# One PSUM pool of eight single banks, scores handled bank by bank, and an order planned from measured lengths, in a windowed-attention, gated-convolution and top-2 expert-attention kernel

## Chip, cores and metric

The kernel runs on one core of a Trainium2 chip. The metric is the device time of one execution in microseconds (us), as the median of several runs; lower is better. The engines of the core are called by the short names of the profile: PE (TensorE matmul), PEld (its weight loads), DVE (VectorE), ACT (ScalarE), POOL (GpSimd) and SP (SyncE, which here issues the DMAs). PSUM, into which PE writes, has eight banks of 128 partitions by 2 KB, that is 512 fp32 values per partition and bank.

## What is computed

Three steps on arrays of 8 batches, 8 heads, 576 positions and 64 values per head (512 values per position): attention in a window of 64 positions, a gated causal convolution, and four single-head causal attentions ("experts"), of which each position adds up the two with the highest logits.

```python
def _attn_ref(q, k, v):                 # 1: window attention, 8 x 8 x 576 x 64
    scores = np.matmul(q, k.transpose(0, 1, 3, 2)) / np.sqrt(D)
    scores = np.where((rel >= 0) & (rel < 64), scores, -1000000000.0)
    attn = np.exp(scores - np.max(scores, axis=-1, keepdims=True))
    attn = attn / (np.sum(attn, axis=-1, keepdims=True) + 1e-09)
    return np.matmul(attn, v)
def _moe_ref(x, w_val, conv_w, w_out):  # 2: x is 8 x 576 x 512
    for k in range(5):
        gate_pre += conv_w[k][None, None, :] * xp[:, k:k + S, :]
    gate = 1.0 / (1.0 + np.exp(-gate_pre))
    return gate * (x @ w_val) @ w_out
def _moe2_ref(x, w_gate, wq, wk, wv, wo):  # 3: E = 4 experts, 2 chosen
    topk = np.argpartition(-(x @ w_gate), 2, axis=-1)[..., :2]
    for e in range(E):
        scores = causal(scale * ((x @ wq[e]) @ (x @ wk[e]).transpose(0, 2, 1)))
        a = softmax(scores)             # with + 1e-9 in the denominator
        out += (weight of e, where chosen) * (a @ (x @ wv[e]) @ wo[e])
```

## The kernel before, in words

**Tiles and stages.** The positions of each batch are cut into five tiles (four of 128 rows and one of 64), so there are 40 tiles. Each tile goes through five functions, whose stages have short names that the text uses:

- front loads q, k and v (tiles raw and rv) and takes the largest magnitude of v (am, L593), from which a batch gets its scales.
- attn1 transposes q and k (qt, L669) and evicts them to qT and kT (qe); splits v into a high and a low fp16 half (vs, vh, vl) and copies the overlap of two tiles (vb); computes the banded scores (sp: the mask by L728, the fp32 products by L730); takes the maxima (mx, L737, negated); exponentiates head by head (ex, L744); splits the result into two fp16 halves in tile Phl (ph L275 or L279, pl L282); transposes it by DMA into PT; multiplies by v (pv, L795), normalises (xn), transposes (xt, L833) and evicts to xT (fp32) and xs (two fp16 halves, xh and xl).
- conv_gate makes the convolution on POOL (cv, L865 to L876: five products with the taps, four additions), tanh on ACT (th, L885), the product with w_val on PE (val, 48 matmuls at L894 to L896: high by high, low by high, high by low), the gate (gv, L902) and its two fp16 halves gs (gh, gl L911).
- proj multiplies by the prepared weights wproj (qk L927 to L929, 48 matmuls; v3 L945 to L947), evicts q3 and k3 (h3), V3 (v3h, v3l) and the logits (tile w4), and finds the two chosen experts and their weights by some ten small steps on DVE (rt, L997 to L1033).
- attn2 computes the causal scores of two or four experts at a time (s3, L1076), maxima (m3, L1085), exponentials with their sums (x3, L1090), the row factors (f3, L1099 and L1103), the two fp16 halves in tile P3hl (ph3 and pl3), the DMA transpose into P3T, the product with V3 (y, L1156), its two fp16 halves ys (yh on ACT L275, yl on DVE L282), the product with wo (o, L1181 to L1183 and L1177), the eviction to tile ot (ot, L275) and the store (st).

Ahead of and beside the first tiles, weights() turns the weights into scaled fp16 pairs. Since `gate * val @ w_out` goes linearly into the four experts, w_out is multiplied by wq, wk, wv and the gate weights once (L485 to L489) and only the product wproj is used. Each of the eight 128x512 pieces of w_val and w_out passes three steps on DVE (L372 to L374), one on ACT (L379) and two on POOL (L387, L388; called the guard here). 36 triples of idle matmuls (fill, L1204) stand at the lowest urgency wherever PE would wait, and 16 more follow the last scores.

**PSUM.** Eight banks are shared out to three kinds of tile: sc, two tiles of two banks each (scores of both attentions), tr, two single banks (transposes, and the outputs of pv and y), and pj, two single banks (the outputs of val, qk, v3, o, and fill).

**What sets the order.** Nothing is scheduled by the compiler: each engine works through its own list in order. The lists come from class Plan. Every stage of every tile is entered with its possible engines and lengths, what it reads and writes, and an urgency: `start[n] + OFF[stage] * STRETCH - BOOST`, with start from a period II = 14109.34 ns per tile. Plan.order then simulates a machine with these lengths and with as many buffers of each name as BUFS says, always takes the operation that can start first (and, among equals, the most urgent), and the operations are written out in the order of the simulated starts. The lengths come from formulas (dv, sa, pl, mm), with a charge of 1500 for choosing DVE and 500 for ACT where either can do it. A tile name in BUFS with the number 1 has one buffer, so that its next user waits for all readers of the last: before, Phl, PT and ot have one, P3hl, kT (a whole batch's keys) and ys two, q3, P3T and w4 three.

## Time and profile before

| | us |
|---|---|
| median of three runs (lowest to highest) | 673.25 (671.52 to 673.39) |
| span of the profiled execution | 668.4 |
| outside the span, against the median | 4.85 |
| PE busy in the span | 622.3 (93%) |
| DVE busy | 554.8 (83%) |
| ACT busy | 509.9 (76%) |
| POOL busy | 487.1 (73%) |

The span runs from the first to the last instruction of one profiled execution, which has no time of its own beside it on the page; so the 4.85 us are the median less the span. Busy time counts an instruction from its start to its end. On PE and DVE one instruction begins before the one ahead of it has ended, so the durations of neighbours overlap, and busy time is the time in which at least one is running. What an added or removed instruction is worth is therefore read from the distance between two starts, and a wait shorter than such an overlap isn't seen as idle time at all.

### The profile page before, as it was taken

What the parts mean: (1) busy time and instruction counts of PE and PEld (TensorE: products, weight loads), DVE (VectorE), ACT (ScalarE), POOL (GpSimd) and SP (SyncE); (2) the same over time, 40 slices, a digit from 0 to 9 for tenths busy, and PEclk for the clock granted to TensorE, in tenths of its full rate; (3) what the DMA queues carried; (4) which work ended last, traced back from release to release, by engine and by line L of the source; (5) the groups of instructions that cost most, each with busy time, mean ns of one, the idle gap of its engine ahead of it and who ended that gap; (6) DMA issues with size and microseconds to landing.
All of it is one profiled execution on the core that took longest, in us unless ns stands there. A gap on an engine that the chain in (4) does not pass through costs nothing. (4 is left out here: it accounts for less than half of the span.)

```text
span 668.4 us, 25309 instructions
## 1 busy us (share of the span) xinstructions
PE 622.3 (93%) x10241; PEld 486.1 (73%) x10253; DVE 554.8 (83%) x1663; ACT 509.9 (76%) x1320; POOL 487.1 (73%) x549
## 2 busy tenths in 40 slices
PE   8999979888989999999999999999999999998996
PEld 3556768777777777877887778877878788776753
DVE  9578788878879889888898989898888978986782
ACT  3568568977878868888788878888879788875662
POOL 6287798995977888669948895789768797867000
PEclk9999999989999999999999999999999999998999
DMA  9769645887796989598887789679647465644256
GB/s 256 197 180 233 153 92 113 205 153 121 134 223 115 170 138 216 124 170 141 169 185 159 126 181 190 142 145 172 151 110 154 97 128 103 110 104 97 50 118 128
DMA packets 306530, 99.44 MB, mean 149 GB/s; under 512 B 294362, under 2 KB 296942, under 8 KB 306414
## 3 DMA queue, kind: packets, MB, share of 16 engines
q1 hardware_dynamic: 306414, 97.84, 71.8%
q8 instruction: 80, 1.31, 0.8%
q14 instruction: 36, 0.29, 0.1%
HBM read 34.63 MB, written 9.44 MB: 66 GB/s over the span
## 5 line engine op out<-in xcount | busy, mean ns | idle before, releaser
L876 POOL TENSOR_TENSOR acc<-acc,ctmp 128x512 f32<-128x512 f32 (+1 forms) x160 | 186.6, 1166 | 6.3
L874 POOL TENSOR_TENSOR ctmp<-xT,cw 128x512 f32<-128x512 f32 (+1 forms) x160 | 152.4, 973 | 0.0
L744 ACT ACTIVATE sc<-sc,mx 128x128 f32<-128x128 f32 x288 | 98.7, 343 | 19.6 <-DVE mx L737 11.1
L894 PE MATMUL pj<-xs,wval 128*128 128x128 f16 (+1 forms) x640 | 101.9, 217 | 3.6 <-ACT k L275 1.4
L895 PE MATMUL pj<-xs,wval 128*128 128x128 f16 (+1 forms) x640 | 101.7, 217 | 0.0
L896 PE MATMUL pj<-xs,wval 128*128 128x128 f16 (+1 forms) x640 | 101.7, 216 | 0.0
L927 PE MATMUL pj<-gs,wproj 128*128 128x128 f16 (+1 forms) x640 | 99.6, 214 | 1.4 <-ACT ot L275 1.4
L928 PE MATMUL pj<-gs,wproj 128*128 128x128 f16 (+1 forms) x640 | 99.5, 214 | 0.0
L929 PE MATMUL pj<-gs,wproj 128*128 128x128 f16 (+1 forms) x640 | 99.5, 214 | 0.0
L1090 ACT ACTIVATE sc<-sc,mx 128x128 f32<-128x128 f32 (+3 forms) x144 | 76.0, 528 | 26.2 <-DVE mx L1085 23.4
L865 POOL TENSOR_TENSOR acc<-xT,cw 128x512 f32<-128x512 f32 (+1 forms) x34 | 34.3, 1010 | 73.7 <-issue 37.5
L282 DVE SCALAR_TENSOR_TENSOR P3hl<-sc,mx,P3hl 128x128 f16<-128x128 f32 (+3 forms) x144 | 75.3, 573 | 10.7 <-ACT P3hl L275 10.5
L275 ACT ACTIVATE P3hl<-sc,mx 128x256 f16<-128x256 f32 (+4 forms) x143 | 69.4, 558 | 9.9 <-DVE mx L1103 3.8
L1076 PE MATMUL sc<-k,q 64*128 64x128 f32 (+5 forms) x384 | 66.6, 450 | 5.5 <-DVE Phl L282 2.8
L691 POOL TENSOR_TENSOR VA<-rv,VA 128x512 f16<-128x512 f32 (+1 forms) x40 | 45.0, 1134 | 30.5 <-ACT VA L275 27.1
L895 PEld LDWEIGHTS <-wval 128*128 128x128 f16 x640 | 62.3, 99 | 3.2 <-issue 2.8
L894 PEld LDWEIGHTS <-wval 128*128 128x128 f16 x640 | 62.3, 99 | 2.9 <-DVE w L1033 1.2
L1085 DVE TENSOR_REDUCE mx<-sc 128x4 f32<-128x512 f32 (+3 forms) x64 | 61.7, 966 | 2.7 <-PE sc L1076 2.2
L927 PEld LDWEIGHTS <-wproj 128*128 128x128 f16 x640 | 61.4, 98 | 1.8 <-issue 0.7
L928 PEld LDWEIGHTS <-wproj 128*128 128x128 f16 x640 | 61.3, 98 | 1.7 <-issue 1.3
L896 PEld LDWEIGHTS <-wval 128*128 128x128 f16 x640 | 62.4, 99 | 0.0
L929 PEld LDWEIGHTS <-wproj 128*128 128x128 f16 x640 | 61.3, 98 | 0.0
(198 smaller groups left out, 1731.9 us busy)
## 6 DMA issues: line engine op xcount, KB each, us to landing
VB<-VA SPq DMA_DIRECT2D x64, 132.0 KB, 2.8
raw<-in_q SPq DMA_DIRECT2D x32, 256.0 KB, 3.5
rv<-in_v SPq DMA_DIRECT2D x32, 256.0 KB, 4.1
raw<-in_k SPq DMA_DIRECT2D x32, 256.0 KB, 3.8
out<-ot SPq DMA_DIRECT2D x32, 256.0 KB, 2.6
w<-in_moe_w_val SPq DMA_DIRECT2D x4, 512.0 KB, 4.0
w<-in_moe_w_out SPq DMA_DIRECT2D x4, 512.0 KB, 3.7
rv<-in_v SPq DMA_DIRECT2D x8, 128.0 KB, 3.7
```

The source lines that it names most:

```text
L275: ac.activation(o, i, AF.Copy, scale=scale)
L282: ve.scalar_tensor_tensor(o, i, scale, hi, op0=OP.mult, op1=OP.subtract)
L744: ac.activation(ps[:, i, :], ps[:, i, :], AF.Exp, bias=t[:, hh:hh + 1])
L874: po.tensor_mul(y, x[:, :, t + i:t + i + T], W["cw"][:, :, t + i:t + i + 1].to_broadcast([128, 4, T]))
L876: po.tensor_add(acc[:, :, :T], acc[:, :, :T], y)
L894: pe.matmul(p[:, m, :T], lhsT=w0, rhs=xs[:, 0, c, :T], start=c == 0, stop=False)
L895: pe.matmul(p[:, m, :T], lhsT=w0, rhs=xs[:, 1, c, :T], start=False, stop=False)
L896: pe.matmul(p[:, m, :T], lhsT=w1, rhs=xs[:, 0, c, :T], start=False, stop=c == 3)
L927: pe.matmul(p[:, m, :T], lhsT=w0, rhs=gs[:, 0, c, :T], start=c == 0, stop=False)
L928: pe.matmul(p[:, m, :T], lhsT=w0, rhs=gs[:, 1, c, :T], start=False, stop=False)
L929: pe.matmul(p[:, m, :T], lhsT=w1, rhs=gs[:, 0, c, :T], start=False, stop=c == 3)
L1090: ac.activation(ps[:, x], ps[:, x], AF.Exp, bias=mx[:, x:x + 1], accum_out=mx[:, 4 + x:5 + x])
```

## The change

**PSUM.** The three kinds become one pool, ps, of eight single banks. Only the planner knows of a limit per use: at most four banks for scores (qs), three for transposes, pv and y (qt), three for val, qk, v3, o and fill (qj).

**Scores bank by bank.** sp and s3 write two single banks where they wrote a tile of two. Maxima, fp16 halves and row factors are then made for each bank by itself, and the planner may put other work between the two; ex becomes one planner operation per head. The last tile of a batch, whose s3 scores are 576 wide, has 512 in one bank and 64 in the other, and two small steps that join the maxima (m3c) and the sums (f3s).

**Keys per tile.** kT holds the keys of one tile instead of a batch (three buffers). A product of sp that reaches over two tiles becomes two of 64 columns: 28 matmuls in place of 20 in the middle tiles of a batch, 20 in place of 12 in the last, 10 as before in the first.

**Buffers.** Phl, PT and ot go from one to two, P3hl, ys and kT to three, P3T to four, q3 to five, w4 to eight; ctmp goes from two tiles of 128x512 to one four times as large.

**Convolution, routing, guard.** Two taps become one POOL instruction of 1024 values, their sums another, and two additions join them to the first tap: six instructions per tile in place of nine, over as many values; the first tap is always on POOL (before, six of 40 tiles had it on ACT). The routing's addition of 1e-9 goes into its last step. vh is always on ACT. All guards are one step on DVE (L440 of the changed kernel), none is on POOL.

**Planner.** The lengths are constants per stage. Latencies (OV, WAIT), a window (NEAR) within which urgency decides among operations that could start, a table of some 900 corrections to the urgency (PRIO, by stage, by stage and tile in the batch, and by tile), a charge of 103.9 for DVE and of -147.2 for ACT, and II = 13700 replace the old numbers.

```diff
-BUFS = dict(raw=5, rv=9, qT=2, kT=2, VA=4, VB=2, Phl=1, PT=1, xn=2, xT=3, xs=2, acc=2, ctmp=2, gs=5,
-           P3hl=2, P3T=3, V3=7, q3=3, k3=2, ys=2, ot=1, am=2, scs=3, w4=3, sc=2, tr=2, pj=2,
-           w64=3, t1=3, wbig=1, ab=4, wp=1, wcat=1)
+BUFS = dict(raw=5, rv=9, qT=2, kT=3, VA=4, VB=2, Phl=2, PT=2, xn=2, xT=3, xs=2, acc=2, ctmp=1, gs=5,
+            P3hl=3, P3T=4, V3=7, q3=5, k3=2, ys=3, ot=2, am=2, scs=3, w4=8, ps=8,
+            w64=3, t1=3, wbig=1, wp=1, wcat=1)
...
+LIMIT = dict(qs=4, qt=3, qj=3)
-II = 14109.34
+II = 13700.0
...
+        's3': 101843.2, ('s3', 0): -2019.0, 'm3': 107663.2, ('m3', 0): 26351.9, 'x3': 144300.6, ('x3', 0): 507958.6, 'f3': -50072.1,
...
-BIAS = dict(DVE=1500.0, POOL=0.0, ACT=500.0)
+BIAS = dict(DVE=103.9, POOL=0.0, ACT=-147.2)
+OV = dict(PE=168.0, DVE=85.0, ACT=110.0, POOL=42.0)
+WAIT = dict(PE=146.0, DVE=34.0, ACT=34.0, POOL=100.0, SP=60.0)
...
+                    if j and (last or not x):
+                        w2 = ((o[:, 0:64], qq, T_["kT", n - 1][rs, m, 64:128]), (o[:, 64:128], qq, kT[rs, m, 0:64]))
+                    else:
+                        w2 = ((o, qq, kT[rs, m]),)
...
-        def mx():
-            T_["mx", n] = t = pool.tile([128, 8], F32, name="mx", bufs=5)
-            ve.tensor_reduce(t[:, :NH].rearrange("p (a b) -> p a b", a=2), s1v(), axis=AX.X, op=OP.max, negate=True)
+        def mx(r):
+            if ("mx", n) not in T_:
+                T_["mx", n] = pool.tile([128, 8], F32, name="mx", bufs=5)
+            ve.tensor_reduce(T_["mx", n][:, 4 * r:4 * r + NQ], T_["s1p", n, r][:, :NQ], axis=AX.X, op=OP.max, negate=True)
...
-        def pl_():
-            hl = T_["Phl", n]
-            residual(by_bank(hl[:, 1, :NH]), by_bank(s1v()), by_bank(hl[:, 0, :NH]), PS)
+        def pl_(r):
+            residual(part1(1, r), flat(T_["s1p", n, r][:, :NQ]), part1(0, r), PS)
...
+            xs = bass.AP(tensor=x.tensor, offset=x.offset + t, ap=[x.ap[0], [1, 2], x.ap[1], [1, T]])
+            ws = bass.AP(tensor=w.tensor, offset=w.offset + t, ap=[w.ap[0], [1, 2], w.ap[1], [0, T]])
+            po.tensor_mul(T_["ctmp", n][:, t - 1:t + 1, :, :T], xs, ws)
...
-            ps = bank(("s3p", n, g), [128, 1024])
+            ps = [bank(("s3p", n, g, u), [128, 512]) for u in (0, 1)]
```

**PE, the product o after its y.** These are the rows up to the first matmul of an o, in the middle of each list. Before, the rows in front of o belong to a val; the y that it needs lies hundreds of matmuls ahead.

```order
L895 LDWEIGHTS wval
L895 MATMUL pj<-xs,wval 128x128
L896 LDWEIGHTS wval
L896 MATMUL pj<-xs,wval 128x128
L1181 LDWEIGHTS ys
L1181 MATMUL pj<-wo_133,ys 128x512
```

After, at a place where y (L1240) of the same tile stands directly ahead: its last matmul, then the end of a small s3 (L1127), then o (L1265).

```order
L1240 LDWEIGHTS V_5_111
L1240 MATMUL ps<-P3T,V_5_111 64x128
L1127 MATMUL ps<-k_4830,q_5945 64x512 x2
L1127 MATMUL ps<-k_4830,q_5945 64x64 x2
L1127 LDWEIGHTS identb
L1127 MATMUL ps<-caus,identb 64x64
L1265 LDWEIGHTS ys
L1265 MATMUL ps<-wo_133,ys 128x512
```

Between the end of y and the first matmul of o, in which time ACT and DVE have to make ys, stood 287 to 448 matmuls in 30 of the 40 tiles; in the changed list there are 7 to 589, at most 30 in 11 tiles and at most 60 in 18.

**DVE, the scores of the window attention.** Before, the maxima of a tile's eight heads are one instruction over two banks (mx<-sc, L737), here next to the maxima of an s3 (L1085), a qT eviction and the routing of a tile (tile w).

```order
L1006 TENSOR_TENSOR pj<-pj,before 128x4x4
L1007 TENSOR_REDUCE pj<-pj 128x4
L737 TENSOR_REDUCE mx<-sc 128x8
L1085 TENSOR_REDUCE mx_6082<-sc 128x2
L279 TENSOR_SCALAR qT<-tr 128x512
L1015 SCALAR_TENSOR_TENSOR w_6004<-pj,w_6004 128x4
L846 TENSOR_TENSOR xs<-tr,xs 128x512
```

After, the maxima (L785) and the low halves (Phl, L332) come in two instructions of one bank each, with the gate (L955, L964), ys and xs between them.

```order
L785 TENSOR_REDUCE mx<-ps 128x4 x2
L332 SCALAR_TENSOR_TENSOR ys<-ps,ys 128x2x64
L329 TENSOR_SCALAR Phl<-ps 128x512
L332 SCALAR_TENSOR_TENSOR Phl<-ps,Phl 128x512
L955 SCALAR_TENSOR_TENSOR ps<-acc,ps 128x512
L332 SCALAR_TENSOR_TENSOR Phl<-ps,Phl 128x512
L785 TENSOR_REDUCE mx<-ps 128x4
L964 TENSOR_TENSOR gs<-ps,gs 128x512
L893 TENSOR_TENSOR xs<-ps,xs 128x4x64
```

The list of DVE grows from 1625 to 1855 rows, most of them such halves.

**The last piece of w_out, on POOL and on DVE.** Before, its guard is two instructions on POOL (L387, L388), between those of other pieces and the splitting of v.

```order
L387 TENSOR_SCALAR w_557<-w_557 128x512
L388 TENSOR_TENSOR t_613<-w_557,t_613 128x512
L589 MEMSET am 128x5
L387 TENSOR_SCALAR w_611<-w_611 128x512
L388 TENSOR_TENSOR t_656<-w_611,t_656 128x512
L691 TENSOR_TENSOR VA_102<-rv,VA_102 64x8x64
```

After, it is one instruction on DVE (L440), behind the three steps of the conversion (L422 to L424), with the scale of wo (so) between them.

```order
L422 TENSOR_SCALAR t_920<-w_780 128x512
L423 SCALAR_TENSOR_TENSOR t_920<-w_780,t_920 128x512
L424 SCALAR_TENSOR_TENSOR t_920<-w_780,t_920 128x512
L578 COPY cm<-ps 128x1
L382 TENSOR_SCALAR so<-cm 128x1
L383 TENSOR_SCALAR cscr<-so 128x1
L384 TENSOR_SCALAR so<-cscr 128x1
L387 TENSOR_SCALAR iso<-so 128x1
L785 TENSOR_REDUCE mx<-ps 128x4
L329 TENSOR_SCALAR wo_133<-w_592,so 128x512
L440 SCALAR_TENSOR_TENSOR t_920<-w_780,t_920 128x512
```

The POOL guards of all pieces leave POOL's list, and the load of that piece moves on SP's list from row 25 to row 43, behind 18 more issues.

## Rows read from the trace of the kernel before

**Rows 1.** The page: busy us, share of the span, instructions, per engine.

```profile
PE 622.3 (93%) x10241; PEld 486.1 (73%) x10253; DVE 554.8 (83%) x1663; ACT 509.9 (76%) x1320; POOL 487.1 (73%) x549
```

**Rows 2.** Windows: stretch, length, busy us (instructions) per engine, PE clock, DMA share, GB/s.

```profile
0.00:91.30 91.30, 81.20 (x686) 51.22 (x693) 69.42 (x141) 50.74 (x102) 61.65 (x68) 1.00 0.80 200
91.30:636.50 545.20, 517.24 (x9245) 422.55 (x9250) 469.22 (x1471) 444.36 (x1181) 424.96 (x478) 0.99 0.72 142
212.50:570.10 357.60, 346.44 (x6229) 280.51 (x6233) 314.29 (x976) 299.46 (x792) 285.64 (x320) 1.00 0.77 151
636.50:668.40 31.90, 23.83 (x314) 12.35 (x311) 16.18 (x53) 14.85 (x37) 0.47 (x4) 0.96 0.60 120
```

**Rows 3.** Timeline of PE, middle of val: start, duration (us), instruction.

```profile
339.15 0.23 PE L894 MATMUL pj<-xs,wval 128*128 128x128 f16 x1
339.21 0.22 PE L895 MATMUL pj<-xs,wval 128*128 128x128 f16 x1
```

**Rows 4.** Waits of PE, 91.3 to 636.5: waiting, awaited, total us, times, longest.

```profile
PE tr L795 <- DMA PT<-Phl: 2.9, 4, 1.2
PE sc L1076 <- DVE Phl L282: 2.8, 3, 1.3
PE tr L1156 <- DMA P3T<-P3hl: 2.8, 2, 2.4
...
PE sc L728 <- DVE P3hl L282: 1.4, 2, 1.2
PE pj L927 <- ACT ot L275: 1.4, 2, 1.1
PE pj L894 <- ACT k L275: 1.4, 3, 0.7
...
PE pj L894 <- ACT ot L275: 1.2, 1, 1.2
PE tr L1156 <- DVE xs L846: 1.0, 2, 0.5
```

**Rows 5.** Timeline of PE, an sp of a middle tile: mask, then products.

```profile
343.96 0.41 PE L728 MATMUL sc<-band_middle,twice 64*64 64x512 bf16 x4
344.20 1.04 PE L730 MATMUL sc<-kT,qT 64*64 64x128 f32 x32
```

**Rows 6.** Timeline of DVE: neighbours of 512 columns, and neighbours of 1024.

```profile
330.62 0.66 DVE L911 TENSOR_TENSOR gs<-pj,gs 128x512 f16<-128x512 f32 x1
331.20 0.41 DVE L846 TENSOR_TENSOR xs<-tr,xs 128x256 f16<-128x256 f32 x1
...
338.43 1.22 DVE L282 SCALAR_TENSOR_TENSOR Phl<-sc,Phl 128x1024 f16<-128x1024 f32 x1
339.57 1.22 DVE L1085 TENSOR_REDUCE mx<-sc 128x4 f32<-128x1024 f32 x1
```

**Rows 7.** Timeline, the last piece of w_out: load, guard, first qk.

```profile
45.62 0.35 SPq L364 DMA_DIRECT2D w<-in_moe_w_out  x1
...
55.89 1.97 POOL L387 TENSOR_SCALAR w<-w 128x512 f32<-128x512 f32 x1
57.94 1.30 POOL L388 TENSOR_TENSOR t<-w,t 128x512 f32<-128x512 f32 x1
...
91.31 0.22 PE L927 MATMUL pj<-gs,wproj 128*128 128x128 f16 x1
```

**Rows 8.** Waits of DVE, whole span.

```profile
DVE ys L282 <- ACT ys L275: 14.1, 13, 6.1
```

**Rows 9.** The chain that ended last, in order of time: start, us, what.

```profile
649.71 5.01 DMA P3T<-P3hl
...
656.17 3.58 DMA out<-ot
...
659.86 0.70 ACT ot L275
...
661.19 1.44 PE tr L1156 x60
```

More of the change, by code (lines that the diff above doesn't have):

```diff
@@ L110, in order @@
                 succ[d].append(i)
+        wait = [min(WAIT[x[0]] for x in o[1]) for o in self.ops]
         avail = [0.0] * n
[L112 removed]
         freed = {}
[L114 removed]
+        free = dict(PE=3300.0, DVE=5300.0, ACT=4300.0, POOL=1700.0, SP=700.0)
+        hw, cold, since, was = 0.0, COLD, set(), "f"
         ready = {i for i in range(n) if not missing[i]}
[L116 removed]
+        out = []
         while ready:
[L118 removed]
+            found = []
             for i in ready:
[L120 removed]
+                _, engs, fn, deps, use, svc = self.ops[i]
                 t, need = avail[i], {}
                 for key in use:
[L123 to L125 removed]
+                    if key not in since:
                         need[key[0]] = need.get(key[0], 0) + 1
@@ L1083, in m3 @@
-        def m3(g):
-            T_["mx3", n, g] = mx = late().tile([128, 12], F32, name="mx3", bufs=6)
-            ve.tensor_reduce(mx[:, :NX], view(g), axis=AX.X, op=OP.max, negate=True)
-        def x3(g):
-            mx, ps = T_["mx3", n, g], view(g)
-            for x in range(NX):
-                ac.activation(ps[:, x], ps[:, x], AF.Exp, bias=mx[:, x:x + 1], accum_out=mx[:, 4 + x:5 + x])
-        def part(g, i):
-            return T_["P3hl", n, g][:, i * wt:i * wt + w0].rearrange("p (x w) -> p x w", x=NX)
+        NU = 1 if last else NX // 2
@@ new lines, in parts3, with m3 @@
+        def parts3(g, u):
+            if last:
+                return ((u, 0, (0, 512)[u], (512, 64)[u]),)
+            return tuple((x, x % NU * pitch, x * wd, wd) for x in range(u * NU, u * NU + NU))
+        def m3(g, u):
+            if ("mx3", n, g) not in T_:
+                T_["mx3", n, g] = late().tile([128, 12], F32, name="mx3", bufs=6)
+            xs = parts3(g, u)
+            ps = T_["s3p", n, g, u]
+            v = ps[:, :xs[0][3]] if NU == 1 else ps.rearrange("p (x w) -> p x w", x=NU)[:, :, :wd]
+            ve.tensor_reduce(T_["mx3", n, g][:, u * NU:u * NU + NU], v, axis=AX.X, op=OP.max, negate=True)
@@ L1110, in pz3, with ph3 @@
+        def ph3(e, g, u):
+            if ("P3hl", n, g) not in T_:
+                new(("P3hl", n, g), [128, 2048], F16, late())
+            for h, l, p, f in split3(g, u):
+                copy(e, h, p, f)
         def pz3(g):
@@ L1113, in pz3, with pl3 @@
             po.memset(hl[:, 640 + 576:1280], 0.0)
[L1115 to L1117 removed]
+        def pl3(g, u):
+            for h, l, p, f in split3(g, u):
+                residual(l, p, h, f)
         def P3T(g):
@@ L1144, in y @@
+            if last:
+                op("pz", n, (("POOL", 170.0),), lambda g=g: pz3(g), r=[("P3hl", n, g, 0, 0)], w=[("P3hl", n, g, 2)])
+            op("P3T", n, (("SP", 900.0 + 50.0 * (2 * wt // 128)),), lambda g=g: P3T(g),
+               r=[("P3hl", n, g, i, u) for i in (0, 1) for u in (0, 1)] + ([("P3hl", n, g, 2)] if last else []),
+               w=[("P3T", n, g)], svc=160.0 * 2 * wt / 128)
         def y():
```

577 lines of the change are left out of this document (271 added, 306 removed), and 83 rows, old and new, of the table PRIO.

## The prediction

> **What bounds the kernel now.** I read the busy times first. PE is busy for 622.3 of 668.4 us, DVE for 554.8, and no other engine for more than 510 [rows 1]: PE is the bound as long as its work is at hand. Then the windows, cut where the program changes character [rows 2]. Until 91.3 us the weights are prepared and PE lacks 91.30 - 81.20 = 10.1 us (idle matmuls of fill count as busy there). From 91.3 to 636.5 it lacks 545.20 - 517.24 = 28.0 us, 11.2 of them in the five middle batches, each of which takes 357.60/5 = 71.5 us, with 346.44/5 = 69.3 us of busy PE. In the last 31.9 us it lacks 8.1. The granted clock is at its upper level, 2.4 GHz, in all of these (0.96 to 1.00), so no term for the clock stands below. The ceiling follows: if every visible gap vanished, 46 of 668.4 us would go, and no more than what is hidden besides.
>
> Something is hidden. A 128-column matmul lasts 0.22 us, but the next starts 0.06 us after it [rows 3], so a wait of up to 0.16 us between two of them shows as busy time. Each tile has some 13 places where PE starts another kind of work, 520 in all, and each may hide up to that much.
>
> Next, what the visible gaps wait for. In the list of PE's waits the eleven largest rows between 91.3 and 636.5, of which eight are shown, sum to 19.9 us. Six of them are waits for somebody to read a PSUM tile empty: scores behind Phl (2.8) and P3hl (1.4), qk and val behind ot or k in pj (1.4, 1.4, 1.2), y behind xs in tr (1.0), together 9.2 us [rows 4]. The largest others are waits for data, the transposing DMAs above all (2.9 and 2.8) [rows 4]. So about 9.2/19.9 = 46% of the sized waiting is for a bank, and the rest for a result.
>
> **The change, part by part.** *Banks.* Eight banks for anybody take away the waits in which the wrong kind of bank is free. I let the whole bank share go: 0.46 x 28.0 = 13 us. It cannot be under 0, if the waits for data take the places (each gap ends with the last of several things), and not over 28.0, if the new order and the doubled buffers meet the waits for data too. I take 13, since the two DMA rows have prices that more buffers alone don't change. *Hidden waits.* If half of the 520 places hide 0.08 us, that is 21 us; the bank share of it is 9.6. I take -4, between 0 and -15.
>
> *Products of sp.* In 32 tiles, eight products of 128 columns become sixteen of 64: eight matmuls more, of two records each. The 32 records of a middle sp take 1.04 us [rows 5], 0.033 each. Sixteen more at that price cost 0.52 us per tile, 17 us in all; if time goes with the columns, which stay the same, nothing. The nearest row, a 128-column fp16 matmul every 0.06 us [rows 3], speaks for time by columns, but not of pieces this short, so I take a third of the upper end, +6. All of this lies on PE, the bound, and no cover takes it.
>
> *Halves on DVE.* 230 more rows in its list, most of them half an instruction. Two neighbours of 512 columns start 0.58 us apart and two of 1024 start 1.14 us apart [rows 6]: a split costs 2 x 0.58 - 1.14 = 0.02 us by starts and 2 x 0.66 - 1.22 = 0.10 by durations. That makes 5 to 23 us on DVE, of which 357.6/668.4, or 3 to 12 us, fall in the five middle batches, where DVE is busy for 314.3 of 357.6 us [rows 2]: 88% become 89 to 91%. I cost it at nothing: the cover is the 43 us in which DVE idles there. If that cover is too thin, the price is rival two. In return the first half of a tile's scores can be exponentiated while the second is reduced, and each bank comes free by itself; that gain is inside the 13.
>
> Against this edit speaks the Trainium skill, page "Perfetto Trace Analysis", section "Optimizing Scalar/DVE Operations": larger instructions raise the throughput of an engine that is saturated, and a DVE instruction on PSUM carries about 125 ns of its own. By that figure the 230 halves would be an estimated 29 us on DVE instead of my 5 to 23; the starts in [rows 6] put the price near a sixth of the page's. The same section also allows the opposite, breaking instructions up where an engine that isn't saturated makes others wait; which of the two holds at 88% no row here shows.
>
> *Lead-in.* The first qk starts at 91.31, and behind it are the products of w_out. The guard of the last piece of w_out runs on POOL from 55.89 to 59.24, 3.3 us [rows 7]; one DVE instruction of 512 columns costs about 0.6 by [rows 6], so 2.7 us leave that path, if it is the one that sets 91.31. Against it stands the load: issued at 45.62 now, it moves behind 18 more issues of some 0.35 us [rows 7], 6.3 us later at worst. And 8 of the 10.1 idle us could go at best. I take -3, from +6 to -8.
>
> *Tail.* The chain that ended last has a transposing DMA of 5.01 us (P3T) and the store of an ot, 3.58 us, for which the only buffer of ot is awaited before the next ACT eviction, the last y behind it [rows 9]. A second ot lets that 3.58 go, a third P3hl part of the 5.01. What is late next is the arithmetic of the last tile, which is as long as before. I take -5, from 0 to -8.
>
> *At nothing.* POOL's taps: six instructions over the same values as nine, with six tiles' first tap added, on an engine that is busy for 425 of 545 us [rows 2]; the cover is the time of val on PE, since only the gate behind it needs tanh. Were it gone, the first tap would be late by one POOL instruction in each of six tiles. The routing without its addition, vh on ACT, and three-buffered kT have one answer each, nothing within what can be measured (a difference under about 0.3%, 2 us, can't be told from no change).
>
> *The sum.* -13 - 4 + 6 - 3 - 5 = -19. The span would be 668.4 - 19 = 649.4; the median is 4.85 above the span and I leave it so: 654 us. Its own range, 645 to 667, comes from moving the two largest unknowns, the bank share and sp, by some 10.
>
> **Rivals.** *One, deeper:* the new order also takes the waits for data, because it is planned with other lengths and there are second buffers for Phl and PT. Then all 28.0 us go, and 8 in the lead-in: 673.25 - 28 - 4 + 6 - 8 - 5 = 634. For it: half of the sized waits have buffers among their causes. Against it: no gap in a list of some 520 starts would be left.
>
> *Two, no change: DVE gives the gain back.* Should the halves cost 0.10 each, the middle batches hold 314.3 + 12 = 326 us of DVE; in five periods of 68.7 us, which the forecast has, that is 95%, and an in-order engine that full makes PE wait about as often as the banks did. The 17 us of the banks and hidden waits come back, and the result is 654 + 17 = 671, with a little more, 673. For it: 14.1 us in 13 waits of DVE for ys, the longest 6.1 [rows 8], show that its queue already stalls on ACT. Against it: the price by starts is 0.02. The rule of the Trainium skill on saturated engines ("Perfetto Trace Analysis", "Optimizing Scalar/DVE Operations") would give this outcome.
>
> *Three, slower: o meets ys late.* In the changed list 11 tiles have at most 30 matmuls between y and o, and 18 at most 60, where before nearly all had hundreds. PE works in order, so when o's ys isn't ready, everything behind it waits, however many banks are free. Behind y come an ACT eviction and then a DVE residual, and the wait of the latter for the former has a mean of 14.1/13 = 1.1 us and a longest of 6.1 [rows 8]. Thirty 128-column matmuls cover 30 x 0.06 = 1.8 us. With 1.8 us uncovered in the eleven tightest tiles and 1.1 in the other seven, 20 + 8 = 28 us are added: 654 + 28 = 682, own range 674 to 700. It decides as soon as the new waits exceed the 19 gained. For it: every other stage was moved by the same table, and any of them may be as tight. Against it: the rows between y and o in such places are often scores, whose 512-column fp32 products are longer than 0.06 apart, and ACT and DVE may have nothing ahead of ys at that moment.
>
> *Four, the change doesn't do what it says:* a limit known only to the planner might be outrun on the chip, so that bank waits stay. That gives 673 - 1 at best, and I count it with rival two.
>
> **How the numbers follow.** Chances: the forecast 0.50, deeper 0.15, no change 0.13, slower 0.22. The predicted time is the forecast's, 654. The range leaves out the lower half of rival one and the upper half of rival three: 637 to 684 holds 0.50 + 0.06 + 0.13 + 0.12, some 0.8. Faster by over 2 us means below 671.2: forecast and rival one with 0.65, and 0.05 of rival two, 0.70. Within 2 us: 0.05 of rival two and 0.02 of rival three, 0.07. Slower: the rest, 0.03 and 0.20, 0.23.
>
> **What would show it.** Banks: among PE's waits between the first qk and the last batch, rows released by Phl, P3hl, ot, k and xs shrink below 2 us together, and the middle period is 68 to 70 us. The products of sp: an sp of a middle tile takes 1.0 to 1.5 us. DVE: busy under 91% in the middle, and the maxima of 512 columns start 0.58 apart. Lead-in: the first qk before 90. Tail: no wait for ot in the last chain. The forecast is wrong if PE's waits for ys, Phl or xs as data are among its largest rows (rival three), if DVE is above 94% in the middle (rival two), or if PE idles under 8 us between the first qk and the last batch (rival one).

## Result and profile after

| | before | changed |
|---|---|---|
| median of five runs, us | 671.58 (669.55 to 673.39) | 664.17 (662.65 to 665.62) |
| ratio, 95% interval | | 0.990 (0.9867 to 0.9932) |
| span of the profiled execution | 668.4 | 660.9 |

The change makes the kernel faster by 1.0%, where 654 us, or 2.9%, had been forecast. The sign was right and 664 lies in the range; of the 19 us that were forecast, 7.4 came. The executions measured here take 1.7 to 2.2 us more than their own spans, most of them 1.8, so of the 4.85 us that the forecast put around the span some 3 were only this: the profiled execution of the kernel before was faster than its median.

The page of the changed kernel first, with the busy us, share and instructions per engine; it answers to [rows 1]:

```profile
PE 628.3 (95%) x10759; PEld 495.4 (75%) x10765; DVE 585.5 (89%) x1893; ACT 483.0 (73%) x1363; POOL 447.8 (68%) x417
```

Then its windows, with the columns of [rows 2], cut at the first and the last qk; the kernel before, cut at its own first and last qk, stands behind it.

```profile
0.00:102.60 102.60, 90.24 (x817) 58.28 (x823) 85.92 (x170) 52.41 (x115) 36.69 (x46) 0.95 0.79 183
102.60:635.30 532.70, 518.10 (x9662) 425.96 (x9661) 484.08 (x1672) 416.80 (x1213) 410.67 (x368) 1.00 0.78 144
635.30:660.90 25.60, 19.96 (x289) 11.13 (x284) 15.48 (x53) 13.74 (x37) 0.47 (x4) 0.94 0.73 150
```

```profile
91.30:637.90 546.60, 518.64 (x9293) 423.95 (x9297) 470.59 (x1474) 444.89 (x1183) 424.96 (x478) 0.99 0.72 142
637.90:668.40 30.50, 22.43 (x270) 10.95 (x266) 14.81 (x50) 14.31 (x35) 0.47 (x4) 0.95 0.62 125
```

Read the second number of each line, the length. The middle fell from 546.6 to 532.7 us (-13.9) and the tail from 30.5 to 25.6 (-4.9), but the lead-in grew from 91.3 to 102.6 (+11.3). The sum is the -7.5 us of the spans. PE's idle time in the middle (length less busy) fell from 28.0 to 14.6.

PE's largest waits in the middle, with the columns of [rows 4]:

```profile
PE ps L1240 <- DMA P3T<-P3hl: 2.4, 3, 1.3
PE ps L844 <- DMA PT<-Phl: 2.1, 6, 0.7
PE ps L981 <- DVE gs L964: 1.8, 2, 1.6
PE ps L719 <- ACT qT L325: 1.7, 1, 1.7
PE ps L998 <- DVE P3hl L332: 1.3, 2, 1.0
```

Of the bank waits, 9.2 us in [rows 4], 4.4 us are left in the new list: the last two rows here, and 1.4 us more of qt (L719) behind k and P3hl. The forecast wanted them under 2. The DMA waits stay on top; all of them together were 5.7 us before and are 6.8 now. So the bank waits give 4.8 of the 13.4 us by which PE idles less, and most of the rest comes from other waits for DVE and ACT, such as these two of the kernel before for a result, which have no counterpart in the new list:

```profile
PE tr L833 <- DVE mx L1099: 2.4, 1, 2.4
...
PE tr L1156 <- ACT sc L1090: 1.3, 1, 1.3
```

In its length, though, the middle went as forecast. What had not been forecast is the lead-in.

### Where the lead-in lost its time

DVE was busy for 58.3 us of the first 80 before and for 71.6 of them after: the guards came to it, and from 50 to 80 us it was busy for 29.7 of 30 us. Around the last piece of w_out, the rows of the timelines of SP, POOL, DVE and PE, each ahead of the next (start, duration, instruction):

```profile
61.08 0.34 SPq L414 DMA_DIRECT2D w<-in_moe_w_out  x1
...
71.91 2.09 POOL L919 TENSOR_TENSOR ctmp<-xT,cw 128x1024 f32<-128x1024 f32 x1
...
74.07 2.69 POOL L923 TENSOR_TENSOR ctmp<-ctmp 128x1024 f32<-128x1024 f32 x1
...
72.15 2.40 DVE L440 SCALAR_TENSOR_TENSOR t<-w,t 128x512 f32<-128x512 f32 x1
74.47 2.85 DVE L332 SCALAR_TENSOR_TENSOR wo<-w,so,wo 128x512 f16<-128x512 f32 x1
...
80.44 0.68 DVE L327 COPY wbig<-ps 128x512 f32<-128x512 f32 x1
...
77.35 0.68 PE L536 MATMUL ps<-wcat,wbig 128*128 128x256 f32 x2
81.26 0.56 PE L535 MATMUL ps<-wgt,wbig 128*128 128x4 f32 x2 [3.23 <-ACT ps L790]
81.68 1.20 PE L536 MATMUL ps<-wcat,wbig 128*128 128x256 f32 x2
...
86.52 4.14 PE L539 MATMUL ps<-wcat,wbig 128*128 128x512 f32 x8
...
102.62 0.23 PE L980 MATMUL ps<-gs,wproj 128*128 128x128 f16 x1
```

Four things are to be seen. The load is issued at 61.08, 15.5 us later than in [rows 7]. The guard, one DVE instruction that had been priced at 0.6 us, takes 2.40. Behind it the two low halves of wo (the first of them 2.85) stand ahead of the eviction of the last transposed piece (80.44). And PE, which needs that eviction, is idle for 3.23 us, after which the same product takes 1.20 us in place of 0.68. The last two rows are the last product with w_out and the first qk. (The row at 81.26 names an ACT instruction as the releaser; the eviction ended at 81.12 and is what came last.) The window tells why it takes longer, with the granted clock third from the right:

```profile
80.00:90.00 10.00, 8.74 (x23) 6.17 (x24) 4.51 (x10) 4.82 (x15) 0.24 (x2) 0.66 0.28 54
```

0.66 is a mean of the two levels: for most of these ten microseconds PE ran at 1.2 GHz. The experiments ask which of these things sets the first qk.

### The profile page after: what moved, and what is told of

It reads as the page before. It is cut to its first block, busy times and chain, and to the rows that moved or that the text cites. A ratio compares the mean times of both kernels' runs of the same rounds, so it can differ in the third digit from the quotient of the medians.

```text
span 660.9 us, 26500 instructions
## 1 busy us (share of the span) xinstructions
PE 628.3 (95%) x10759; PEld 495.4 (75%) x10765; DVE 585.5 (89%) x1893; ACT 483.0 (73%) x1363; POOL 447.8 (68%) x417
## 5 line engine op out<-in xcount | busy, mean ns | idle before, releaser
L919 POOL TENSOR_TENSOR ctmp<-xT,cw 128x1024 f32<-128x1024 f32 (+1 forms) x80 | 139.8, 1762 | 53.5 <-ACT xT L325 45.3
L790 ACT ACTIVATE ps<-ps,mx 128x128 f32<-128x128 f32 x288 | 91.8, 365 | 23.5 <-DVE mx L785 20.3
L981 PE MATMUL ps<-gs,wproj 128*128 128x128 f16 (+1 forms) x640 | 100.9, 215 | 1.8 <-DVE gs L964 1.8
L980 PE MATMUL ps<-gs,wproj 128*128 128x128 f16 (+1 forms) x640 | 101.3, 216 | 0.0
L982 PE MATMUL ps<-gs,wproj 128*128 128x128 f16 (+1 forms) x640 | 100.9, 215 | 0.0
L947 PE MATMUL ps<-xs,wval 128*128 128x128 f16 (+1 forms) x640 | 99.6, 214 | 0.2 <-DVE xn L859 0.2
L949 PE MATMUL ps<-xs,wval 128*128 128x128 f16 (+1 forms) x640 | 99.4, 214 | 0.0
L948 PE MATMUL ps<-xs,wval 128*128 128x128 f16 (+1 forms) x640 | 99.4, 214 | 0.0
L1152 ACT ACTIVATE ps<-ps,mx 128x512 f32<-128x512 f32 (+4 forms) x160 | 80.1, 503 | 24.3 <-DVE mx L1143 15.1
L927 POOL TENSOR_TENSOR acc<-acc,ctmp 128x512 f32<-128x512 f32 (+1 forms) x80 | 94.0, 1175 | 4.0
L923 POOL TENSOR_TENSOR ctmp<-ctmp 128x1024 f32<-128x1024 f32 (+1 forms) x40 | 85.8, 2146 | 0.7
L332 DVE SCALAR_TENSOR_TENSOR P3hl<-ps,mx,P3hl 128x512 f16<-128x512 f32 (+4 forms) x160 | 81.6, 536 | 2.7 <-ACT P3hl L325 2.3
L1143 DVE TENSOR_REDUCE mx<-ps 128x1 f32<-128x512 f32 (+4 forms) x128 | 67.2, 556 | 4.7 <-PE ps L1127 4.4
L1127 PE MATMUL ps<-k,q 64*128 64x128 f32 (+5 forms) x384 | 66.6, 451 | 0.2 <-ACT k L325 0.2
```

Of the source, the lines that this page charges most:

```text
L332: ve.scalar_tensor_tensor(o, i, scale, hi, op0=OP.mult, op1=OP.subtract)
L790: ac.activation(x, x, AF.Exp, bias=T_["mx", n][:, 4 * r + i:4 * r + i + 1])
L919: po.tensor_mul(T_["ctmp", n][:, t - 1:t + 1, :, :T], xs, ws)
L923: po.tensor_add(y[:, 0:2], y[:, 0:2], y[:, 2:4])
L927: po.tensor_add(acc, acc, T_["ctmp", n][:, i, :, :T])
L947: pe.matmul(p[:, m, :T], lhsT=w0, rhs=xs[:, 0, c, :T], start=c == 0, stop=False)
```

## Experiments on the lead-in

**Only the load earlier (l_load).** Theory A: the late load sets the lead-in. Theory B: DVE's list does.

```diff
+    BUFS['w64'] = 4
+    move(('w64', 8), lambda: at(('w64', 7)) + 1)
```

> The changed kernel with one instruction moved: the load of the last piece of w_out is issued right behind that of the third piece, into a fourth buffer; every other instruction stays in its place. In the changed kernel it was issued at 61.1 us (45.6 before) and the first qk started at 102.6 (91.3 before). Theory A (the late load sets the lead-in): the first qk comes 8 to 11 us earlier and the time falls by 6 to 9 us, to about 656. Theory B (the list of DVE paces the lead-in; when the load landed DVE still had other work ahead of the conversion): the first qk stays within 1 us of 102.6 and the time within 2 us of 664.

Measured 0.9897 of before (0.9858 to 0.9935), as the changed kernel; first qk 104.8 us, not earlier. Theory A falls: 15 us of a late load cost nothing, since its conversion stands behind other work on DVE anyway.

**The low halves of wo later on DVE (l_wolate).**

```diff
+    for turn in (0, 1):
+        move(('W', 'o'), lambda: max(x for x, o in enumerate(seq) if ('W', 'p') in o[2]) + 1)
```

> The changed kernel with two DVE instructions moved: the two low halves of wo (4.5 us between 74.5 and 79.0, ahead of the DVE eviction of the last transposed piece of w_out at 80.4) come behind the low halves of wproj. Theory B (DVE's list paces the lead-in): that eviction comes about 4.5 us earlier, PE's gap of 3.2 us before its next product goes and with it the stretch at the lower clock (0.66 between 80 and 90 us); the first qk starts 4 to 7 us earlier and the time falls by 3 to 6 us, to 658 to 661. Theory A (the load): nothing there depends on wo, so the first qk is as late as before within 1 us.

Measured 0.9911 (0.9878 to 0.9944): no gain, though the first qk came at 97.4 us, 5.2 earlier, as theory B said. At the third qk 0.6 of the 5.2 was left (123.9 against 124.5). The rows of DVE there, and of PE behind the first qk:

```profile
96.57 4.72 DVE L333 SCALAR_TENSOR_TENSOR wo<-w,so,wo 128x512 f16<-128x512 f32 x2
101.22 0.68 DVE L956 SCALAR_TENSOR_TENSOR ps<-acc,ps 128x512 f32<-128x512 f32 x1
101.81 0.15 DVE L676 COPY mb<-ps 128x1 f32<-128x1 f32 x1
...
102.01 0.27 PE L999 MATMUL ps<-wproj,gs 128*128 128x260 f16 x1 [1.71 <-DVE mb L676]
```

The same 4.7 us now hold up the tile work: PE waits 1.71 us for a bank whose reader (mb) stands behind them. Here, moving work about on a full engine moved the wait with it.

**All guards on POOL (l_poolguard).**

```diff
+    seq[:] = [(fn, 'POOL' if fn.__code__.co_name == 'guard' else e, what) for fn, e, what in seq]
```

> The changed kernel with all nine guards of the weights on POOL again (two instructions each, as before the change) at their old places in the order. Theory B1 (the guards on DVE, 0.68 to 2.4 us each, are the part of DVE's list that delays the lead-in): DVE is freed of 9 us before 80 us, the first qk starts 4 to 9 us earlier and the time falls by 3 to 7 us. Rival (POOL's taps stand ahead of the later guards, 3.3 us each on POOL): the last three guards of w_out come later than on DVE, the first qk is 0 to 6 us later and the time up to 5 us longer.

Measured 0.9904 (0.9871 to 0.9937), first qk at 101.0: 1.6 us earlier, between the figures of the two theories. DVE's busy time before the first qk fell from 85.9 to 74.7 us, and it was of hardly any use: POOL's guards come behind its taps, and the last one ends at 79.5, where DVE's ended at 74.5.

**The low halves of wo on POOL (l_wopool, wopool2), and what is left then.**

```diff
+        def wolow(c):
+            x = T_["w64", "o"][:, c]
+            po.tensor_mul(x, x, so.to_broadcast([128, 512]))
+            po.tensor_sub(wout2[:, 1, c], x, wout2[:, 0, c])
...
-            wop((("DVE", dv(512)),), lambda c=c: residual(wout2[:, 1, c], T_["w64", "o"][:, c], wout2[:, 0, c], so),
+            wop((("DVE", dv(512)),), lambda c=c: wolow(c),
```

> The changed kernel with the two low halves of wo made on POOL (a product and a difference each, 4.4 us in all) behind the low halves of wproj, so that they are on DVE's list nowhere. When they were only moved on DVE, the first qk came 5.2 us earlier and the gain was gone two tiles later. Theory (DVE is full from 50 to 105 us, so only work taken off its list counts): the first qk comes 5 us earlier, as there, and at least 3 us of it are still there at the third qk (124.5 us in the changed kernel) and in the time: 660 to 662. Rival (something else holds the tiles behind the first qk, a load or a transpose): the third qk is again within 1 us of 124.5 and the time within 2 us of 664.

Measured 660.08 us (657.36 to 663.61), 0.981 of before (0.976 to 0.986), with the first qk at 96.1 and the third at 118.0, 6.5 us earlier than in the changed kernel (124.5): this time the gain stays. Once more, beside the changed kernel on one chip:

> The kernel with the low halves of wo on POOL once more. Theory (its lead is real and comes from the lead-in): 0.978 to 0.985 of before and 0.5% to 1.2% under the changed kernel of the same call; first qk 96 us. Rival (the first set of runs was lucky): within 0.4% of the changed kernel.

> The changed kernel once more, instruction for instruction, beside the next two. Expected 0.987 to 0.993 of before, and in the second look at its trace: first qk 102 to 105 us, tail 25.6, PE's idle time between the first and the last qk 15 to 20 us (14.6 in the first look, 18 to 20 in the looks at kernels with the same order there).

Measured 0.986 (0.9802 to 0.9919) for it and 0.992 (0.989 to 0.9949) for the changed kernel: again the faster one, by 0.6%, though the intervals of this second set overlap. It is the fastest version here that computes everything. Its windows, with the changed kernel's of the same set of runs behind:

```profile
0.00:96.10 96.10, 85.77 (x817) 55.48 (x823) 81.37 (x168) 52.66 (x115) 40.74 (x50) 1.00 0.89 195
96.10:629.80 533.70, 516.65 (x9661) 424.19 (x9659) 484.02 (x1672) 417.47 (x1213) 410.80 (x368) 1.00 0.79 144
```

```profile
0.00:104.80 104.80, 92.63 (x817) 60.09 (x823) 86.43 (x170) 52.19 (x115) 36.54 (x46) 0.93 0.76 179
104.80:640.90 536.10, 518.07 (x9663) 425.19 (x9662) 484.10 (x1672) 417.17 (x1213) 410.78 (x368) 1.00 0.79 144
```

The lead-in is 8.7 us shorter here and its clock is 1.00 in place of 0.93; the middle has the same instructions and about the same length. The second profile of the changed kernel has 18.0 us of idle PE in the middle, so 14.6 was a low one; in the nine profiles of the kernels of this section, which have the same order there, it lies between 17 and 22.

Where the gain comes from can be read beside the rows above. The last product with w_out and the first qk of the kernel with wo on POOL:

```profile
80.59 3.60 PE L540 MATMUL ps<-wcat,wbig 128*128 128x512 f32 x8
...
96.15 0.23 PE L985 MATMUL ps<-gs,wproj 128*128 128x128 f16 x1
```

That product ends at 84.19 here and at 90.66 in the changed kernel, and in both 11.96 us pass from there to the first qk; the same 11.96 stand in every kernel of this section but the last. The transposes of the last piece end at the same time in both (75.5 and 75.4). So the 6.5 us lie between the two: 3.2 are the wait for the eviction, and the rest, some 3 us, are products that ran at the lower clock after it.

With the guards of w_out left out as well:

> As the kernel with the low halves of wo on POOL, and the guards of the four pieces of w_out (which set values of very small magnitude to zero) are left out, so that DVE has some 6 us less to do before 75 us. Theory (DVE's list): the first qk comes 8 to 14 us earlier than in the changed kernel, near 90 as before the change, and the time falls by 5 to 10 us, to 654 to 659: the forecast of 654 was wrong by the lead-in alone. Rival (the first qk isn't what the time hangs on): the first qk comes earlier, the time stays within 2 us of that of the kernel with wo on POOL.

Measured 0.9802 (0.9749 to 0.9855), first qk 94.9, 7.7 us earlier than in the changed kernel and not the 8 to 14 of the theory: the guards of w_out cost 1.2 us of the lead-in and nothing that the time can tell. With the guards on POOL instead:

> The kernel with the low halves of wo on POOL (660.1 us, ratio 0.981), and all guards of the weights on POOL as before the change. Leaving the guards of w_out out moved the first qk only from 96.1 to 94.9 us. Theory (once wo is off DVE's list, what DVE does there beside the guards is late anyway): first qk 94 to 97 us, time within 2 us of 660. Rival (DVE's list is still the bound, and POOL is free enough to take 9 us more): first qk 90 to 93 us and 655 to 658.

Measured 0.989 (0.984 to 0.9941), first qk 100.3: outside what either theory gave, and the whole gain is lost. The last guard ends at 78.9 on POOL, where it ended at 74.6 on DVE; that is late for PE whatever DVE is spared.

**Taps of 512 values (l_taps).** This run asks why DVE's guard took 2.40 us.

```diff
-            po.tensor_mul(T_["ctmp", n][:, t - 1:t + 1, :, :T], xs, ws)
+            for u in (0, 1):
+                po.tensor_mul(T_["ctmp", n][:, t - 1 + u, :, :T], x[:, :, t + u:t + u + T], w[:, :, t + u:t + u + 1].to_broadcast([128, 4, T]))
```

> The kernel with the low halves of wo on POOL, and the taps and their sums on POOL again as instructions of 512 values (two in place of each of 1024, same order). In the changed kernel DVE instructions of the weights' conversion that begin beside a POOL instruction end about one duration of their own after that instruction's end (the guard at 72.15 lasts 2.40 us in place of 0.68, behind a tap sum that ends at 73.99). Theory (such a DVE instruction waits for the POOL instruction that is running): with taps of about 1.1 us the longest of these DVE instructions fall from 2.4 to at most 2.0 us, DVE's lengthening before 105 us from 11.7 to 8 to 10 us, the first qk 0 to 2 us earlier. Rival (the two merely share bandwidth): the lengthening stays within 1 us of 11.7, since as many values are moved. In both POOL is busier by some 30 us over the run, and the time within 4 us of 660.

Measured 0.9843 (0.9794 to 0.9892), first qk 97.8. The same guard:

```profile
73.60 1.53 DVE L441 SCALAR_TENSOR_TENSOR t<-w,t 128x512 f32<-128x512 f32 x1
```

1.53 in place of 2.40; but another step, which was to take at most 2.0 us as well, took longer than any in the changed kernel:

```profile
53.43 5.17 DVE L424 SCALAR_TENSOR_TENSOR t<-w,t 128x512 int32<-128x512 int32 x1
```

It begins inside one POOL instruction, three more follow that one without a gap, and it ends 0.55 us behind the last of them. Counted against the shortest instruction of the same line and shape, all DVE instructions before 105 us are lengthened by 11.9 us here, against 13.1 and 13.8 in the two profiles of the kernel with wo on POOL (the expectation's 11.7 for the changed kernel doesn't come out of this count, which gives 15.9), and the first qk came no earlier. That a running POOL instruction holds up such a DVE instruction fits the rows: 72.15 + 2.40 = 74.55 is 0.55 us behind the tap's end at 74.00, and so is the end of each of the ten such instructions of 128x512 in the changed kernel. Shorter taps alone don't shorten the lead-in. What the taps cost by way of wo, this run can't tell, since wo is on POOL in it: of the 4.6 us that the two low halves took on DVE (2.85 and 1.75), 1.5 are their own length (twice 0.74) and 3.1 the wait for POOL.

**The whole chain of w_out earlier (q_adv20).**

```diff
+    key = {i: (x - 20 if i in early else x) for x, (e, i) in enumerate(line)}
+    for e, i in line:
+        if i in early:
+            key[i] = max([key[i]] + [key[d] + 1e-3 for d in plan.ops[i][3]])
```

> The kernel with the low halves of wo on POOL, and all steps of w_out's chain (loads, conversions, guards, transposes, products, scales, halves of wproj) written out 20 places earlier in the common order, as far as what they need allows; nothing else moves. 20 places are about 4.5 us there. Theory (the lead-in is a matter of order: DVE and PE would have had time for the chain earlier): first qk at 90 to 94 us, time 2 to 5 us under the kernel with wo on POOL, 655 to 658. Rival (the chain already waits for engines, not for its place): first qk stays at 95 to 97 and the time within 2 us of that kernel; what was put behind is late instead.

Measured 681.26 us, 1.0148 (1.0086 to 1.021), with the first qk at 119.6. SP's largest waits before it, the rows of the guard and of the load at which the second of them ends, and the windows:

```profile
SPq L815 <- DVE Phl L333: 24.4, 3, 14.6
SPq L415 <- DVE cm L573: 13.8, 1, 13.8
SPq L415 <- DVE t L441: 7.3, 1, 7.3
```

```profile
71.51 3.52 DVE L441 SCALAR_TENSOR_TENSOR t<-w,t 128x512 f32<-128x512 f32 x1 [4.12 <-ACT w L430]
...
75.06 0.34 SPq L415 DMA_DIRECT2D w<-in_moe_w_out  x1
```

```profile
0.00:119.60 119.60, 97.29 (x817) 62.75 (x823) 75.41 (x170) 52.97 (x115) 40.45 (x51) 0.89 0.74 159
119.60:657.80 538.20, 521.07 (x9663) 428.06 (x9661) 483.68 (x1671) 417.62 (x1212) 408.58 (x367) 0.99 0.76 143
```

A load of w_out (L415) now stands on SP's list where no buffer is free, and waits 13.8 us. (The row names cm, the next on DVE; the guard, which reads a buffer of w, ends at 71.51 + 3.52 = 75.03, just ahead of the load at 75.06.) The tiles' loads and transposes behind it wait too. The miss is the most telling of the runs: the lead-in grew by 23.5 us against the kernel with wo on POOL (96.1), the middle by 4.5, and the span by 28.1. That pair of profiles is an unlucky one, the slowest of four executions against one of the fastest of six; by the ratios of the same set, 1.0148 against 0.986, the loss is 19 us. So most of what the lead-in loses comes out at the end.

## Experiments on the middle and the tail

**PSUM as before, under the new order (m_pair, m_44).** In m_pair the scores have two tiles of two banks, and the other four banks are for all else; in m_44 there are four single banks for scores and four for all else. The edit of m_44:

```diff
-        return new(key, shape, dtype, psum, "ps")
+        use = "qs" if QUOTA[key[0]] == "qs" else "qo"
+        T_[key] = t = psum.tile(shape, dtype, name=use, bufs=4)
+        return t
```

> The changed kernel in its own order with PSUM nearly as before the change: scores in two tiles of two banks, each given back as a whole, and the other four banks for all else. Theory (the gain in the middle is that of the banks): PE's idle time between the first and the last qk, 14.6 us in the changed kernel and 28.0 before, grows by 8 to 25 us, and the time by about as much, to 672 to 690. Rival (the gain is that of the order and the lengths behind it): idle time grows by less than 4 us and the time stays within 3 us of 664.

> The changed kernel in its own order, with PSUM in two pools of four single banks, one for scores and one for all else, neither lending to the other. With scores in tiles of two banks as well it took 741 us. Theory (lending is what the one pool gives): PE's idle time between the first and the last qk grows from 14.6 us to 25 to 40 and the time to 675 to 690. Rival (what matters is that a score bank is given back by itself; lending is little): idle time grows by under 5 us, time within 4 us of 664.

Measured 740.74 us, 1.1019 (1.0982 to 1.1056), and 683.32 us, 1.0147 (1.01 to 1.0193). The middle of each:

```profile
110.60:711.50 600.90, 530.22 (x9654) 430.53 (x9659) 490.03 (x1670) 434.77 (x1211) 410.46 (x368) 0.99 0.69 128
```

```profile
106.20:659.20 553.00, 522.50 (x9659) 428.08 (x9662) 486.49 (x1671) 419.49 (x1212) 410.47 (x368) 0.99 0.76 139
```

PE idles 70.7 and 30.5 us there, against 14.6 to 18.0. So the new order needs both: without lending it is 17 us over its own time of 666, and with pairs of banks 75. Neither run plans the order again for the banks that it has, so what the best order with such banks would take is not shown.

**Lending under the old order (b_lend).**

```diff
-        return new(key, shape, dtype, psum, KIND[key[0]][0])
+        tag = KIND[key[0]][0]
+        T_[key] = t = psum.tile(shape, dtype, name="sc" if tag == "sc" else "one", bufs=2 if tag == "sc" else 4)
+        return t
```

> The kernel before in its own order, with its two pools of two single banks (transposes, projections) joined into one of four; scores keep their two tiles of two banks. Theory (lending by itself is what takes the bank waits): of the six bank waits of the forecast the four that aren't for scores (5.0 us) go, PE's idle time between the first and the last qk falls from 28.0 us to about 23, the time by 3 to 6 us. Rival (banks are worth something only where the order is planned for them): idle time and the time stay within 2 us of before.

Measured 670.51 us, 0.9968 (0.9925 to 1.001): unclear, and at most a small gain. Its middle:

```profile
92.80:637.20 544.40, 517.47 (x9290) 422.96 (x9295) 469.99 (x1473) 443.48 (x1183) 424.59 (x476) 1.00 0.72 142
```

26.9 us of idle time in place of 28.0: the rival's side. But the waits that were to go are still there:

```profile
PE one L1158 <- DVE xs L848: 1.6, 2, 1.1
...
PE one L896 <- ACT ot L277: 1.4, 1, 1.4
...
PE one L929 <- ACT ot L277: 1.1, 1, 1.1
...
PE one L896 <- ACT k L277: 0.9, 2, 0.7
```

They sum to 5.0 us, as before. So a joined pool of four took no bank wait away under the old order, and what that order would gain without these waits isn't shown. The gain of the middle came with the pool and the order together; how it divides between them isn't settled by these runs.

**The split products of sp (m_sp1).**

```diff
-                        w2 = ((o[:, 0:64], qq, T_["kT", n - 1][rs, m, 64:128]), (o[:, 64:128], qq, kT[rs, m, 0:64]))
+                        w2 = ((o, qq, T_["kT", n - 1][rs, m]),)
```

> The changed kernel with each pair of 64-column products of sp replaced by one of 128 columns on the keys of the tile ahead (the keys of the tile itself are left out there): 256 matmuls fewer on PE, all else in its place. Theory (a split product costs by its pieces, as forecast at +6 us): PE's time in sp falls from 52.6 to 47 us, and the time by 3 to 6 us, to 658 to 661. Rival (time goes by columns, or other engines fill the place): sp falls by under 2 us, or the time by under 2.

Measured 667.37 us, 0.9898 (0.9835 to 0.996). The products of a middle tile take 1.20 us in the changed kernel:

```profile
97.86 1.20 PE L780 MATMUL ps<-kT,qT 64*64 64x64 f32 x48
```

against 1.04 in [rows 5], 0.16 us more per tile or 5 us in 32 tiles. In this kernel, which leaves out part of the keys, PE's time in sp falls by 4.5 us (5.6 had been expected), but the time doesn't follow; the interval, 1.2% wide, can't exclude 3 us. So the price on PE is shown, and whether the time pays it is open.

**Two buffers for ot, three for P3hl, in the kernel before (b_tail).**

```diff
+    BUFS.update(ot=2, P3hl=3)
```

> The kernel before in its own order, with two buffers for ot in place of one and three for P3hl in place of two, and nothing else. Theory (the tail's gain in the change, 30.5 to 25.6 us from the last qk to the end, is that of these buffers, as forecast): the tail shrinks by 3 to 6 us, the waits for ot before val and qk go (2.6 us in the middle), and the time falls by 4 to 8 us, ratio 0.988 to 0.994. Rival (the tail's gain is that of the order): the tail stays within 1.5 us of 30.5 and the time within 2 us of before.

Measured 672.57 us, 0.998 (0.995 to 1.001), which can't be told from no change; the tail is 28.7 us, where the change had brought it from 30.5 to 25.6. The two waits for ot in the middle are still there, with 2.8 us. The chain of the changed kernel's end, with the columns of [rows 9]:

```profile
649.64 0.70 ACT P3hl L325
...
651.26 3.38 DMA P3T<-P3hl
...
655.83 0.97 PE ps L1261 x12
```

The store of ot is gone from the chain and the transposing DMA takes 3.38 us in place of 5.01; with the buffers alone the DMA in the chain still takes 4.98. So these two buffers are worth 1.8 of the tail's 4.9 us in that profile; the rest came with the other parts of the change, which no run tells apart.

## Why the prediction was right or wrong

PE's time by kind of work is counted here from each matmul's start to the start of the next, or to its own end where that is earlier, over each whole stretch. The second row is what the others leave of the middle's 13.9 us; no row shows that it is hidden waits.

| step | forecast | measured |
|---|---|---|
| visible idle time of PE, middle | -13 | -13.4 (28.0 to 14.6; to 18.0 in a second profile) |
| other work in the middle, where hidden waits are | -4 | -4.4 |
| sp, whole run | +6 | +5.9 (48.7 to 54.6), of which products +4.4 and masks +1.4 |
| tail | -5 | -4.9 |
| lead-in, without sp | -3 | +9.4 |
| sum, of the spans | -19 | -7.5 |

- **The step that failed is the lead-in.** It was priced by one path, the guard's change of engine (2.7 us gained), with a late load as the risk (6.3 us at worst). Both were the wrong things to look at: the load came 15.5 us later, and moving it back changed nothing; the guards of w_out, left out of the kernel with wo on POOL, moved the first qk by 1.2 us. What counted is that DVE, busy for 58.3 of the first 80 us before and for 71.6 after, was taken for idle enough to take the guards, and that the change put 4.6 us of wo ahead of an eviction that PE waited for. Taken off DVE's list this brought 6.5 to 8.7 us of the first qk back and 0.6 to 0.9% of the time; some half of the gain in the lead-in is the wait itself and half the lower clock behind it, for which the forecast had no term. Of the other 5 us, between 96.1 and 91.3, the cause stays open: not the load, not the guards, not the taps, and not the place of the chain alone. The rows show where they lie: the last piece of w_out is transposed by 75.5 us, where it was by 64.3 before; by the first qk 5 of these 11 us are left.
- **DVE was costed at nothing with a cover from the middle batches alone.** There the cover held: 484.08 of 532.70 us are 91%, the upper end forecast, and rival two did not come. In the lead-in there was no such cover. [rows 2] showed DVE at 69.4 of 91.3 us there, and the forecast did not put the guards (nine instructions, 11.2 us in all) on top of it.
- **The middle went as forecast in size, in part by luck.** The forecast let 13 us of bank waits go and kept the waits for data. Bank waits fell by 4.8 us, the DMA waits grew by 1.1, and other waits for DVE and ACT gave most of the rest; 14.6 is besides the lowest idle time of all profiles with this order, and with the 18.0 of the second one the fall is 10.0. b_lend and m_44 show that neither a joined pool of four under the old order nor the new order with a divided pool has the gain.
- **The products of sp** took a third of the upper bound, as was guessed; no row had been there for the third. The masks (+1.4) had no term.
- **The tail was right in size and wrong in cause.** The two buffers that were named give a third of it.
- **Rival three** did not come either: the waits of PE for ys sum to 0.4 us, although 11 tiles have at most 30 matmuls between y and o. Its price, taken from DVE's waits for ACT [rows 8], did not carry over to PE.
- **Splitting on DVE.** The rule of the Trainium skill against it ("Perfetto Trace Analysis", "Optimizing Scalar/DVE Operations") would have cost DVE an estimated 29 us. DVE's busy time grew by 30.7 us in all, from 554.8 to 585.5, but that is no measure of it: the guards came, the routing grew shorter, and evictions went from ACT to DVE and back. The groups that were split, maxima and low halves of both attentions, took 225.7 us of busy time in 288 instructions before and take 247.1 in 448 now, 21.4 more; from start to start it is some 12 us more. Both lie within the bounds that were worked out from [rows 6] (5 to 23). The other sentence there, that breaking up may pay where an engine isn't saturated, is not contradicted by the middle, where DVE is at 91%; no run here takes the halves apart from the rest.

## What to carry to other kernels

Price work that is moved to an engine by how full that engine is in the stretch where it lands, and look at what stands behind it on that engine's list; a mean over the run hides a lead-in where it has no room. An early stage through which everything passes is paid for at the end, in both directions and for the greater part: 23.5 us more before the first qk cost 19 us of time here, and 6.5 to 8.7 us less gave 4 to 6. Look for the one instruction that such a stage hangs on: in eight kernels here 11.96 us passed between the last product with w_out and the first qk. And a looser resource and the order have to be made for each other: a joined pool took no wait away under the old order, and a divided one cost 17 to 75 us under the new.

## What the hardware showed that was not expected

In the changed kernel a DVE instruction of 128x512 that reads two operands from SBUF and begins while POOL is at work takes 2 to 4 times as long: 2.40 and 2.85 us in place of 0.68 and 0.74, beside POOL instructions of 2.09 and 2.69 us, and its end comes 0.55 us behind that of the POOL instruction. With POOL's taps half as long the guard took 1.53 us; where POOL's instructions followed each other without a gap, one such step took 5.17. All this stands in the profile as busy time of DVE, not as idle time. The Trainium skill, page "SBUF — State Buffer", section "SBUF: two separate sides", says that a DVE instruction with two SBUF inputs and a POOL instruction that reads SBUF exclude each other for their whole length, whichever comes first. The rows of the changed kernel agree, with DVE as the one that waits; POOL waits too, since a tap, 1.91 us as a rule, takes up to 2.69 where such a DVE instruction was running. The kernel before has an exception: beside the first POOL step of a guard (L387), two such DVE instructions, at 8.66 and 11.90 us, keep their 0.69 us. And a gap of PE of 3.2 us at 78 us was followed by a stretch of 10 us with a granted clock of 0.66, in which a pair of products took 1.20 us in place of 0.68.
